# An FFN of one selected row inside a fused attention kernel: gate, up and h brought to 128 partitions by small DMAs instead of matmuls, the down rows regrouped to fit, and the row chosen two units sooner

## The chip, the cores and the metric

The kernel runs on one core of one Trainium2 chip. The metric is the device time of one execution in microseconds (us). A "unit" below is one tile of 8 matmuls of 512 columns on the matrix engine (PE): 8 x 0.216 = 1.73 us (in the kernel before, 16 such matmuls take 3.45 us from 44.52 to 47.97 us). DVE is the vector engine, ACT the scalar engine, POOL the GpSimd engine and SP the engine that issues most DMAs.

## The reference, cut to what matters

```python
# x: [1, 2048, 1024]; w_gate, w_up: [1024, 3584]; w_down: [3584, 1024]; all bf16
r = x @ w_r                                   # one router logit for each of 2048 tokens
idx = argsort(-r)[:, :1]                      # C = 1: one token is chosen
x_sel = take_along_axis(x, idx)
y = (silu(x_sel @ w_gate) * (x_sel @ w_up)) @ w_down
b = x + scatter(y * sigmoid(r[idx]))          # only the chosen row gets y
a = linear_attention(x, wqkv) @ wo            # 32 heads, phi(t) = where(t > 0, t + 1, exp(t)) + 1e-6
g = sigmoid((x * gate_w).sum(-1))
out = g * a + (1 - g) * b
```

Nearly all the arithmetic is attention on PE. The FFN works on one row, but has to read 22 MB of weights. So it is laid beside the attention: DVE and PE use the weights while PE goes through the key, value and query units.

Of the kernel before, what the change touches and what calls it, by code (L numbers as in the profile page):

```python
# [13 lines left out]
BF = mybir.dt.bfloat16  # L14
# [8 lines left out]
P = 128  # L23
# [10 lines left out]
GU_AFTER = {(7, "end"): 4, (9, 1): 4, (10, 3): 8, (12, 1): 8}  # L34
FLUSH_AFTER = {(9, 3), (13, 0)}
GATE_STEPS = {6: 5, 7: 6, 8: 5}
M_AFTER = {3: (0, 0), 6: (0, 1), 9: (1, 0), 12: (1, 1)}
DOWN_STEPS = {10: (1, 1, 1, 1, 1, 1), 11: (1, 1, 1, 1, 1), 12: (1, 0, 1, 1, 1), 13: (1, 1, 1, 1, 1), 14: (1, 1, 1, 1, 1), 15: (1, 1, 1)}
# [5 lines left out]
def kernel(  # L44
# [113 lines left out]
    sel4 = const.tile([P, 4], BF)  # L158
    nc.gpsimd.memset(sel4[:], 0.0)
    for j in range(4):  # L160
        nc.gpsimd.memset(sel4[32 * j : 32 * j + 1, j : j + 1], 1.0)
# [212 lines left out]
    h_bf = [rt.tile([P, 512], BF, name=f"h_bf{i}") for i in range(2)]  # L374
    sg_t = [rt.tile([P, 512], F32, name=f"sg{i}") for i in range(2)]
# [14 lines left out]
    def finish_gate(half, ps, w):  # L390
        eg = tmp.tile([P, 512], F32, tag="ffn_e", bufs=1)
        act.activation(eg[:, 0:w], ps[:, 0:w], ACTF.Exp, scale=-1.0)
        dve.tensor_scalar_add(eg[:, 0:w], eg[:, 0:w], 1.0)
        dve.reciprocal(eg[:, 0:w], eg[:, 0:w])
        dve.tensor_tensor(sg_t[half][:, 0:w], ps[:, 0:w], eg[:, 0:w], op=ALU.mult)

    def finish_up(half, ps, w):
        dve.tensor_tensor(h_bf[half][:, 0:w], ps[:, 0:w], sg_t[half][:, 0:w], op=ALU.mult)

        def h_transpose():  # L400
            hps = ps_ffn.tile([P, 16], F32, tag="f")
            nb = w // P
            for b in range(nb):
                pe.matmul(hps[:, 4 * b : 4 * b + 4], lhsT=h_bf[half][:, b * P : (b + 1) * P], rhs=sel4[:], start=True, stop=True)
            dst = hcol[:].rearrange("p (j b) -> p j b", b=7)[:, :, 4 * half : 4 * half + nb]
            src = hps[:, 0 : 4 * nb].rearrange("p (b j) -> p j b", j=4)
            dve.tensor_copy(dst, src)

        ffn_state["pending"] = h_transpose

    def gate_up(half, which):
        w = 512 if half == 0 else 384
        for wi in which:
            wmat = (B_w_gate, B_w_up)[wi]
            for c in range(KC):
                def load(wmat=wmat, c=c):
                    return gate_up_load(half, wmat, c)

                def compute(wt, wi=wi, c=c):
                    if c == 0:  # L420
                        ps = ps_ffn.tile([P, 512], F32, tag="f")
                        ffn_state["ps"] = ps
                    ps = ffn_state["ps"]
                    for j in range(4):
                        pe.matmul(ps[32 * j : 32 * j + 32, 0:w], lhsT=xs_pad[:, c, :], rhs=wt[:, w * j : w * j + w],
                                  start=(c == 0), stop=(c == KC - 1), tile_position=(0, 32 * j))
                    if c == KC - 1:
                        (finish_gate, finish_up)[wi](half, ps, w)

                yield load, compute  # L430
# [15 lines left out]
    def gate_reduce():  # L446
# [4 lines left out]
        finish_gate(0, ps, 512)  # L451

    def down_rows():
        wdv = B_w_down.rearrange("(k p) n -> p k n", p=P)
        pairs = [(7 * j + b, 1) for b in (0, 2) for j in range(4)]
        pairs += [(7 * j + 4, 1) for j in range(4)] + [(6, 7), (20, 7)]
        for i2, (k0, dk) in enumerate(pairs):
            def load(k0=k0, dk=dk):
                wt = ffw.tile([P, 2048], BF, tag="ffw")
                ld = nc.sync.dma_start(out=wt[:].rearrange("p (k n) -> p k n", k=2), in_=wdv[:, k0 : k0 + dk + 1 : dk, :])  # L460
# [4 lines left out]
            def compute(wt, kk, i2=i2, k0=k0, dk=dk):  # L465
                w, h1 = wt[:, 1024 * kk : 1024 * kk + 1024], hcol[:, k0 + dk * kk : k0 + dk * kk + 1]
                if i2 == 0 and kk == 0:
# [26 lines left out]
    def ffn_pieces():  # L494
# [5 lines left out]
        for n in (2, 4):  # L500
            yield from islice(dn, n)
            yield from islice(gu, 8)
# [4 lines left out]
    inflight = deque()  # L507

# [6 lines left out]

    def ffn_flush():
        pend = ffn_state.pop("pending", None)
        if pend is not None:
            pend()
# [33 lines left out]

    q_units = deque((g, j) for j in range(4) for g in range(NG))
    for t in range(4):
        unit_KVACC(t)
    for t in range(4, NT):
        for nb in range(4):
# [4 lines left out]
            ffn_step(GU_AFTER.get((t, nb), 0))  # L563
            if (t, nb) in FLUSH_AFTER:
                ffn_flush()
            gate_step(int(nb < GATE_STEPS.get(t, 0)))
            steps = DOWN_STEPS.get(t, ())
            if nb < len(steps):
                down_step(steps[nb])
        for i in range(Q_PER_T[t]):  # L570
            unit_Q(*q_units.popleft())
            gate_step(int(4 + i < GATE_STEPS.get(t, 0)))
            if 4 + i < len(steps):
                down_step(steps[4 + i])
            if t == 4 and i == 0:
                router_part1()
                ffn_prefetch()
        if t == 5:
            router_part2()
        ffn_step(GU_AFTER.get((t, "end"), 0))  # L580
# [167 lines left out]
```

## The kernel before: what the change and the argument touch

One ring of nine 512 KB buffers (`FFN_DEPTH`) takes all the FFN's weights in the order of `ffn_pieces`; a new load is issued when a buffer is free. DVE accumulates the gate's half 0 and all the down rows by scaled adds (`gate_step`, `down_step`, half a buffer at a time); PE does the other gate and up pieces in groups of four or eight (`ffn_step`). Constants say after which unit of the attention what is done. "Half 0" has 4 x 512 of the 3584 hidden columns and "half 1" 4 x 384.

```python
GU_AFTER = {(7, "end"): 4, (9, 1): 4, (10, 3): 8, (12, 1): 8}
FLUSH_AFTER = {(9, 3), (13, 0)}
GATE_STEPS = {6: 5, 7: 6, 8: 5}
DOWN_STEPS = {10: (1, 1, 1, 1, 1, 1), 11: (1, 1, 1, 1, 1), 12: (1, 0, 1, 1, 1), 13: (1, 1, 1, 1, 1), 14: (1, 1, 1, 1, 1), 15: (1, 1, 1)}
FFN_DEPTH = 9
# ... (cut)
    def finish_gate(half, ps, w):          # silu of 128 x w, of whose partitions only 0, 32, 64, 96 matter
        eg = tmp.tile([P, 512], F32, tag="ffn_e", bufs=1)
        act.activation(eg[:, 0:w], ps[:, 0:w], ACTF.Exp, scale=-1.0)
        dve.tensor_scalar_add(eg[:, 0:w], eg[:, 0:w], 1.0)
        dve.reciprocal(eg[:, 0:w], eg[:, 0:w])
        dve.tensor_tensor(sg_t[half][:, 0:w], ps[:, 0:w], eg[:, 0:w], op=ALU.mult)

    def finish_up(half, ps, w):
        dve.tensor_tensor(h_bf[half][:, 0:w], ps[:, 0:w], sg_t[half][:, 0:w], op=ALU.mult)

        def h_transpose():                 # h to 128 partitions by 4 (half 0) or 3 (half 1) matmuls
            hps = ps_ffn.tile([P, 16], F32, tag="f")
            nb = w // P
            for b in range(nb):
                pe.matmul(hps[:, 4 * b : 4 * b + 4], lhsT=h_bf[half][:, b * P : (b + 1) * P], rhs=sel4[:], start=True, stop=True)
            # ... (cut: copy of hps to hcol on DVE)
        ffn_state["pending"] = h_transpose
# ... (cut)
    def down_rows():
        wdv = B_w_down.rearrange("(k p) n -> p k n", p=P)          # row 128k + p on partition p
        pairs = [(7 * j + b, 1) for b in (0, 2) for j in range(4)]
        pairs += [(7 * j + 4, 1) for j in range(4)] + [(6, 7), (20, 7)]
        for i2, (k0, dk) in enumerate(pairs):
            def load(k0=k0, dk=dk):
                wt = ffw.tile([P, 2048], BF, tag="ffw")
                ld = nc.sync.dma_start(out=wt[:].rearrange("p (k n) -> p k n", k=2), in_=wdv[:, k0 : k0 + dk + 1 : dk, :])
                # ... (cut: order of the queue)
                return wt

            def compute(wt, kk, i2=i2, k0=k0, dk=dk):
                w, h1 = wt[:, 1024 * kk : 1024 * kk + 1024], hcol[:, k0 + dk * kk : k0 + dk * kk + 1]
                if i2 == 0 and kk == 0:
                    dve.tensor_scalar(yacc, w, h1, None, op0=ALU.mult)
                else:
                    dve.scalar_tensor_tensor(yacc, w, h1, yacc, op0=ALU.mult, op1=ALU.add)

            yield load, compute
# ... (cut)
    def ffn_pieces():
        g0, u0, gu, dn = gate_rows(), gate_up(0, (1,)), gate_up(1, (0, 1)), down_rows()
        yield from islice(g0, 6)
        yield from islice(u0, 4)
        yield from g0
        yield from u0
        for n in (2, 4):                   # down pieces ahead of each group of half 1
            yield from islice(dn, n)
            yield from islice(gu, 8)
        yield from dn
        yield from wo_pieces()
# ... (cut)
    for t in range(4, NT):
        for nb in range(4):
            unit_KV(t, nb)
            # ... (cut)
            ffn_step(GU_AFTER.get((t, nb), 0))
            if (t, nb) in FLUSH_AFTER:
                ffn_flush()                # the pending h_transpose
            gate_step(int(nb < GATE_STEPS.get(t, 0)))
            steps = DOWN_STEPS.get(t, ())
            if nb < len(steps):
                down_step(steps[nb])
        for i in range(Q_PER_T[t]):
            unit_Q(*q_units.popleft())
            # ... (cut: further steps)
            if t == 4 and i == 0:
                router_part1()             # DVE: index of the row; POOL: fetch of the row
                ffn_prefetch()
        if t == 5:
            router_part2()                 # PE: the row to 128 partitions
        ffn_step(GU_AFTER.get((t, "end"), 0))
        if t == 8:
            gate_reduce()
```

A unit's result leaves its bank of PE's accumulator memory through ACT and then, for a key or a query, through one DVE instruction (`pk` or `pq_all` in the trace). There are four such banks (`ps_work`, `bufs=4`).

## Time and profile before

| | kernel before |
|---|---|
| time, median of 3 runs | 251.46 us (251.42 to 251.52) |
| span of the profiled run | 250.1 us |
| PE busy, granted clock | 244.7 us (98%), 1.00 |
| DVE, ACT, POOL busy | 163.1, 125.8, 51.9 us |
| PE's waits in the whole span | 1.7 us |

PE bounds the kernel; the prediction below shows the lines for that. Here are the page's line of DMA shares in 40 slices (tenths of all 16 DMA engines' time; a slice is 6.25 us), its line on the down loads (14 loads of 512 KB, median 5.8 us from issue to landing), and from the list of waits DVE's wait for down rows (us in total, times, longest):

```profile
DMA  6999990019999928499699996230000564454122
...
wt<-in_B_w_down_dram SPq DMA_DIRECT2D x14, 512.0 KB, 5.8
...
DVE gacc L80 <- DMA wt<-in_B_w_down_dram: 3.7, 3, 1.8
```

The table of windows gives the rate while down rows are loading. Its columns are the stretch, its length, the busy time and count of PE, PEld, DVE, ACT and POOL, then PE's clock, the DMA share and GB/s:

```profile
130.00:135.00 5.00, 5.00 (x28) 2.27 (x27) 4.38 (x7) 3.59 (x6) 1.06 (x2) 1.00 1.05 301
```

The share is at 1.05: all 16 engines work, at a mean of 301 GB/s, and a piece of 512 KB takes 524,288 bytes / 301 GB/s = 1.7 us. By their packets, about 57 of the 301 GB/s are loads of `A_wo` issued by POOL; without them it is 244 GB/s, or 2.1 us a piece. DVE needs a piece every two units, 3.5 us, so the stream is clearly faster than its use and DVE waits only 3.7 us in all.

### The profile page before, as it was taken

Reading aid. Unit: us, or ns where it says so; the run is one execution under the profiler, and the core shown is the slowest. Engines: PE = TensorE matmul, PEld = TensorE weight load, DVE = VectorE, ACT = ScalarE, POOL = GpSimd, SP = SyncE. Lnnn points to the kernel's source line nnn. Section 1 sums busy time; section 2 is a strip of 40 time slices with the busy share of each in tenths; the row PEclk is TensorE's granted clock in tenths of the full one; section 3 lists DMA queues with packets and bytes.
Section 4 is the critical chain, followed back from the end, with each engine's and each line's share of the span. In section 5 each row is a group of like instructions: output and inputs, shape, how many; then the busy total and the mean of one; then the engine's idle time right before and its main releaser. Section 6 shows DMA issues by size and latency. Waiting matters only on the chain.

```text
span 250.1 us, 4197 instructions
## 1 busy us (share of the span) xinstructions
PE 244.7 (98%) x1602; PEld 111.1 (44%) x1602; DVE 163.1 (65%) x257; ACT 125.8 (50%) x200; POOL 51.9 (21%) x102
## 2 busy tenths in 40 slices
PE   7999999999999999999999999999999999999994
PEld 3444454444444434444544444444444444444442
DVE  0045015326999288699689993585878999953442
ACT  2096235556545364564535554568887633333210
POOL 5000001010000100000132000210666689950000
PEclk9999999999999999999999999999999999999999
DMA  6999990019999928499699996230000564454122
GB/s 199 303 340 225 258 334 26 0 27 320 350 348 272 340 58 250 146 338 327 194 292 300 457 349 134 70 132 1 3 0 5 171 210 144 161 175 144 66 84 84
DMA packets 47242, 47.73 MB, mean 191 GB/s; under 512 B 18732, under 2 KB 35380, under 8 KB 47160
## 3 DMA queue, kind: packets, MB, share of 16 engines
q1 hardware_dynamic: 46552, 46.29, 60.7%
q0 software_dynamic: 640, 1.19, 1.8%
q8 instruction: 12, 0.20, 0.3%
q14 instruction: 6, 0.05, 0.1%
q10 hardware_dynamic: 32, 0.00, 0.0%
HBM read 39.34 MB, written 8.40 MB: 191 GB/s over the span
## 4 chain that ended last, share of the span: by engine, by line
PE 95%; DMA 2%; SPq 1%; DVE 0%; issue 0%; DVEq 0%
PE ps L80 88%; PE first L80 2%; DMA wkv<-in_A_wqkv_dram 2%; PE kvacc L80 2%; PE dps L80 1%; PE rps L80 1%; SPq L80 1%; PE pm L80 1%; PE gps L80 0%; DVE ot L80 0%; PE yps L80 0%; PE xs_ps L80 0%; DVEq L743 0%; PE pt L80 0%; PE hps L80 0%
## 5 line engine op out<-in xcount | busy, mean ns | idle before, releaser
L80 PE MATMUL ps<-wkv,xT 128*128 128x512 bf16 x480 | 106.5, 379 | 0.0
L80 PEld LDWEIGHTS <-xT 128*128 128x128 bf16 x512 | 49.3, 98 | 60.5 <-issue 2.6
L80 PE MATMUL ps<-xT,wq 128*128 128x512 bf16 x256 | 58.4, 379 | 0.0
L80 PE MATMUL ps<-m_sb,pq_all 128*128 128x512 bf16 (+2 forms) x264 | 55.6, 373 | 0.0
L80 ACT ACTIVATE u<-ps 128x512 f32<-128x512 f32 x60 | 35.9, 599 | 36.5 <-PE ps L80 35.8
L80 ACT ACTIVATE e<-u 128x512 f32<-128x512 f32 x64 | 40.4, 632 | 2.0
L646 POOL TENSOR_TENSOR pq_all<-pq_all,rb 128x512 bf16<-128x512 bf16 x32 | 36.6, 1163 | 14.4 <-DVE rb L80 13.9
L80 PEld LDWEIGHTS <-pq_all 128*128 128x128 bf16 x264 | 25.5, 98 | 30.2 <-issue 0.4
L80 PEld LDWEIGHTS <-wq 128*128 128x128 bf16 x256 | 24.3, 98 | 30.2 <-issue 2.1
L80 DVE SCALAR_TENSOR_TENSOR pq_all<-ps,e 128x512 bf16<-128x512 f32 x32 | 22.0, 686 | 23.6 <-ACT e L80 23.5
L80 DVE SCALAR_TENSOR_TENSOR gacc<-wt,hcol,gacc 128x1024 f32<-128x1024 bf16 x27 | 34.6, 1281 | 4.1 <-DMA wt<-in_B_w_down_dram 3.7
L80 ACT CAST vt<-ps 128x512 bf16<-128x512 f32 x32 | 18.9, 589 | 32.8 <-PE ps L80 32.8
L80 DVE SCALAR_TENSOR_TENSOR ot<-ps,gate,xg 128x512 bf16<-128x512 f32 (+2 forms) x33 | 23.6, 724 | 15.1 <-PE ps L80 14.2
L80 ACT ACTIVATE xg<-xt,omg 128x1024 f32<-128x1024 bf16 x16 | 18.2, 1148 | 25.8 <-DVE ot L80 25.8
L80 DVE SCALAR_TENSOR_TENSOR pk<-ps,e 128x512 bf16<-128x512 f32 x28 | 19.1, 686 | 7.5 <-ACT e L80 7.5
L209 POOL MEMSET vt<- 128x16 bf16 x16 | 2.4, 200 | 101.8 <-PE kvacc L80 101.3
L80 DVE STREAM_SHUFFLE rb<-rdp 128x512 f32<-128x512 f32 x32 | 22.5, 731 | 0.0
L80 DVE SCALAR_TENSOR_TENSOR gacc<-wt,xs_f,gacc 128x1024 f32<-128x1024 bf16 x14 | 17.4, 1283 | 0.3 <-DMA wt<-in_B_w_gate_dram 0.3
L80 DVE CAST r_bf<-rps 128x512 bf16<-128x512 f32 x1 | 0.7, 692 | 12.6 <-PE rps L80 12.6
L80 DVE SCALAR_TENSOR_TENSOR pk<-first,e 128x512 bf16<-128x512 f32 x4 | 2.8, 692 | 8.4 <-ACT e L80 8.4
L80 PE MATMUL first<-wkv,xT 128*128 128x512 bf16 x32 | 7.4, 379 | 0.2
L80 DVE RECIPROCAL rd<-dn 128x512 f32<-128x512 f32 x2 | 6.7, 3334 | 0.0
(104 smaller groups left out, 88.1 us busy)
## 6 DMA issues: line engine op xcount, KB each, us to landing
wt<-in_B_w_down_dram SPq DMA_DIRECT2D x14, 512.0 KB, 5.8
wt<-in_B_w_gate_dram SPq DMA_DIRECT2D x8, 512.0 KB, 7.2
wt<-in_B_w_up_dram SPq DMA_DIRECT2D x8, 512.0 KB, 8.9
xt<-xp SPq DMA_DIRECT2D x16, 256.0 KB, 2.9
out_dram<-ot SPq DMA_DIRECT2D x15, 256.0 KB, 2.0
wt<-in_B_w_gate_dram SPq DMA_DIRECT2D x8, 384.0 KB, 5.3
wt<-in_B_w_up_dram SPq DMA_DIRECT2D x8, 384.0 KB, 7.5
wkv<-in_A_wqkv_dram SPq DMA_DIRECT2D x8, 256.0 KB, 5.2
```

The costliest lines, as they stand in the source:

```text
L80: inst = fn(*a, **k)
L209: nc.gpsimd.memset(vt_t[t][:, :, :, 64:65], 1.0)
L646: nc.gpsimd.tensor_tensor(sl, sl, rb[:], op=ALU.mult)
```

## The change

Its intent: relieve DVE of the work on 128x512 tiles of which four rows matter, and PE of the seven small transposing matmuls. The rows of gate and up are copied out by ACT, four small DMAs bring them to 128 partitions x 16 (or 12) columns, and silu and the product run on those. A column f of h then stands at another place, so each buffer of down rows has to hold other rows: partition 32j + r takes the rows of column group j that stand together in one stretch of memory. The row is chosen two units sooner, and the plan of steps is shifted to match. The diff, cut to its core:

```diff
-GU_AFTER = {(7, "end"): 4, (9, 1): 4, (10, 3): 8, (12, 1): 8}
-FLUSH_AFTER = {(9, 3), (13, 0)}
-GATE_STEPS = {6: 5, 7: 6, 8: 5}
+GU_AFTER = {(7, 3): 4, (8, "end"): 4, (10, 3): 8, (12, 1): 8}
+GATE_STEPS = {5: (0, 1, 1, 1, 1), 6: (1, 1, 1, 1, 1), 7: (1, 1, 1, 0, 1, 1), 8: (1, 1)}
-DOWN_STEPS = {10: (1, 1, 1, 1, 1, 1), 11: (1, 1, 1, 1, 1), 12: (1, 0, 1, 1, 1), 13: (1, 1, 1, 1, 1), 14: (1, 1, 1, 1, 1), 15: (1, 1, 1)}
+DOWN_STEPS = {9: (0, 0, 0, 1, 1), 10: (1, 1, 0, 0, 1, 1), 11: (1, 1, 1, 1), 12: (0, 0, 1, 1, 1), 13: (1, 1, 1, 1, 2), 14: (1, 1, 1, 1, 1), 15: (1, 1, 1, 1)}
+FINISH_AT = {(9, 2), (11, 0), (12, 4)}
... (cut: finish_gate, finish_up and h_transpose go; sel4 goes)
+    def finish(wi, half, ps):
+        w = 512 if half == 0 else 384
+        n = w // 32
+        act.copy(rows[wi][:, 0:w], ps[:, 0:w])
+        nc.gpsimd.dma_start(out=cols[half][wi][:, 0:n], in_=rows[wi][0:128:32, 0:w])
+        g, u, h = cols[half][0][:, 0:n], cols[half][1][:, 0:n], slice(16 * half, 16 * half + n)
+
+        def silu():
+            e = rt.tile([P, 16], F32, name=f"ffn_e{half}")
+            act.activation(e[:, 0:n], g, ACTF.Exp, scale=-1.0)
+            dve.tensor_scalar_add(e[:, 0:n], e[:, 0:n], 1.0)
+            dve.reciprocal(e[:, 0:n], e[:, 0:n])
+            dve.tensor_tensor(g, g, e[:, 0:n], op=ALU.mult)
+
+        def product():
+            dve.tensor_tensor(h_bf[:, h], u, g, op=ALU.mult)
+            dve.tensor_copy(hcol[:, h], h_bf[:, h])
+
+        late.append((silu, product)[wi])
... (cut)
     def down_rows():
-        wdv = B_w_down.rearrange("(k p) n -> p k n", p=P)
-        pairs = [(7 * j + b, 1) for b in (0, 2) for j in range(4)]
-        pairs += [(7 * j + 4, 1) for j in range(4)] + [(6, 7), (20, 7)]
-        for i2, (k0, dk) in enumerate(pairs):
-            def load(k0=k0, dk=dk):
+        wdv = B_w_down.rearrange("(j f) n -> j f n", j=4)
+        for k in range(0, 28, 2):
+            c0, n, i0 = (0, 16, k) if k < 16 else (512, 12, k - 16)
+
+            def load(c0=c0, n=n, i0=i0):
                 wt = ffw.tile([P, 2048], BF, tag="ffw")
-                ld = nc.sync.dma_start(out=wt[:].rearrange("p (k n) -> p k n", k=2), in_=wdv[:, k0 : k0 + dk + 1 : dk, :])
+                src = wdv[:, c0 : c0 + 32 * n, :].rearrange("j (r i) n -> j r i n", i=n)[:, :, i0 : i0 + 2, :]
+                ld = nc.sync.dma_start(out=wt[:], in_=src.rearrange("j r i n -> j r (i n)"))
... (cut: compute, with hcol's column k + kk)
-        for n in (2, 4):
+        for n in (2, 3):
             yield from islice(dn, n)
             yield from islice(gu, 8)
... (cut: a helper that does the steps of a slot and the late parts of the FFN at FINISH_AT; router_part1 after KV(4,1), router_part2 after KV(5,0))
```

More of the change, by code (lines that the diff above doesn't have):

```diff
@@ L157 @@
     nc.gpsimd.memset(ones_row[:], 1.0)
-    sel4 = const.tile([P, 4], BF)
-    nc.gpsimd.memset(sel4[:], 0.0)
-    for j in range(4):
-        nc.gpsimd.memset(sel4[32 * j : 32 * j + 1, j : j + 1], 1.0)
     off16_i = const.tile([P, 1], I32)
@@ L373 @@
     ffw = phq.enter_context(tc.tile_pool(name="ffw", bufs=FFN_DEPTH, side="right"))
-    h_bf = [rt.tile([P, 512], BF, name=f"h_bf{i}") for i in range(2)]
-    sg_t = [rt.tile([P, 512], F32, name=f"sg{i}") for i in range(2)]
+    rows = [rt.tile([P, 512], F32, name=f"gu_rows{i}") for i in range(2)]
+    cols = [[rt.tile([P, 16], F32, name=f"gu_cols{i}{h}") for i in range(2)] for h in range(2)]
+    h_bf = rt.tile([P, 28], BF)
     ffn_state = {}
@@ L388, in gate_up_load @@
         return wt
-    def finish_gate(half, ps, w):
-        eg = tmp.tile([P, 512], F32, tag="ffn_e", bufs=1)
-        act.activation(eg[:, 0:w], ps[:, 0:w], ACTF.Exp, scale=-1.0)
-        dve.tensor_scalar_add(eg[:, 0:w], eg[:, 0:w], 1.0)
-        dve.reciprocal(eg[:, 0:w], eg[:, 0:w])
-        dve.tensor_tensor(sg_t[half][:, 0:w], ps[:, 0:w], eg[:, 0:w], op=ALU.mult)
-    def finish_up(half, ps, w):
-        dve.tensor_tensor(h_bf[half][:, 0:w], ps[:, 0:w], sg_t[half][:, 0:w], op=ALU.mult)
-        def h_transpose():
-            hps = ps_ffn.tile([P, 16], F32, tag="f")
-            nb = w // P
-            for b in range(nb):
-                pe.matmul(hps[:, 4 * b : 4 * b + 4], lhsT=h_bf[half][:, b * P : (b + 1) * P], rhs=sel4[:], start=True, stop=True)
-            dst = hcol[:].rearrange("p (j b) -> p j b", b=7)[:, :, 4 * half : 4 * half + nb]
-            src = hps[:, 0 : 4 * nb].rearrange("p (b j) -> p j b", j=4)
-            dve.tensor_copy(dst, src)
-        ffn_state["pending"] = h_transpose
+    def finish(wi, half, ps):
[14 more added lines that the diff above has]
+        late.append((silu, product)[wi])
     def gate_up(half, which):
@@ L427, in compute @@
                     if c == KC - 1:
-                        (finish_gate, finish_up)[wi](half, ps, w)
+                        finish(wi, half, ps)
                 yield load, compute
@@ L450, in gate_reduce @@
                       start=True, stop=True, tile_position=(0, 32 * j))
-        finish_gate(0, ps, 512)
+        finish(0, 0, ps)
+        late.rotate(1)
     def down_rows():
-        wdv = B_w_down.rearrange("(k p) n -> p k n", p=P)
-        pairs = [(7 * j + b, 1) for b in (0, 2) for j in range(4)]
-        pairs += [(7 * j + 4, 1) for j in range(4)] + [(6, 7), (20, 7)]
-        for i2, (k0, dk) in enumerate(pairs):
-            def load(k0=k0, dk=dk):
+        wdv = B_w_down.rearrange("(j f) n -> j f n", j=4)
+        for k in range(0, 28, 2):
+            c0, n, i0 = (0, 16, k) if k < 16 else (512, 12, k - 16)
+            def load(c0=c0, n=n, i0=i0):
                 wt = ffw.tile([P, 2048], BF, tag="ffw")
-                ld = nc.sync.dma_start(out=wt[:].rearrange("p (k n) -> p k n", k=2), in_=wdv[:, k0 : k0 + dk + 1 : dk, :])
+                src = wdv[:, c0 : c0 + 32 * n, :].rearrange("j (r i) n -> j r i n", i=n)[:, :, i0 : i0 + 2, :]
+                ld = nc.sync.dma_start(out=wt[:], in_=src.rearrange("j r i n -> j r (i n)"))
                 tc.add_manual_dep(ld.ins, ffn_state["last_ld"].ins.name, NOSYNC, reason="queue order")
@@ L463, in load, with compute @@
                 return wt
-            def compute(wt, kk, i2=i2, k0=k0, dk=dk):
-                w, h1 = wt[:, 1024 * kk : 1024 * kk + 1024], hcol[:, k0 + dk * kk : k0 + dk * kk + 1]
-                if i2 == 0 and kk == 0:
+            def compute(wt, kk, k=k):
+                w, h1 = wt[:, 1024 * kk : 1024 * kk + 1024], hcol[:, k + kk : k + kk + 1]
+                if k + kk == 0:
                     dve.tensor_scalar(yacc, w, h1, None, op0=ALU.mult)
@@ L507 @@
     inflight = deque()
+    late = deque()
     def ffn_prefetch():
@@ L514, in ffn_prefetch @@
             inflight.append((nxt[0](), nxt[1]))
-    def ffn_flush():
-        pend = ffn_state.pop("pending", None)
-        if pend is not None:
-            pend()
     def ffn_step(n):
@@ L552, in down_finish, with slot @@
                             in_=brow[0:128:32, :])
+    def slot(t, i):
+        gu = GU_AFTER.get((t, i), 0)
+        ffn_step(gu)
+        strict[0] = True
+        while late and (t, i) in FINISH_AT:
+            late.popleft()()
+        strict[0] = False
+        for step, plan in ((gate_step, GATE_STEPS), (down_step, DOWN_STEPS)):
+            steps = plan.get(t, ())
+            if i != "end" and i < len(steps):
+                step(steps[i])
     q_units = deque((g, j) for j in range(4) for g in range(NG))
@@ L562 @@
                     unit_KVACC(t0)
-            ffn_step(GU_AFTER.get((t, nb), 0))
-            if (t, nb) in FLUSH_AFTER:
-                ffn_flush()
-            gate_step(int(nb < GATE_STEPS.get(t, 0)))
-            steps = DOWN_STEPS.get(t, ())
-            if nb < len(steps):
-                down_step(steps[nb])
+            if (t, nb) == (4, 1):
+                router_part1()
+                ffn_prefetch()
+            if (t, nb) == (5, 0):
+                router_part2()
+            slot(t, nb)
         for i in range(Q_PER_T[t]):
             unit_Q(*q_units.popleft())
-            gate_step(int(4 + i < GATE_STEPS.get(t, 0)))
-            if 4 + i < len(steps):
-                down_step(steps[4 + i])
-            if t == 4 and i == 0:
-                router_part1()
-                ffn_prefetch()
-        if t == 5:
-            router_part2()
-        ffn_step(GU_AFTER.get((t, "end"), 0))
+            slot(t, 4 + i)
+        slot(t, "end")
         if t == 8:
```

## The prediction

> **What bounds the kernel now.** I read the page's busy shares and slices first, then the list of what the matrix engine (PE) waited for, then the timeline of PE alone, then the groups of the vector engine (DVE). The first two parts of the page:
>
> ```profile
> PE 244.7 (98%) x1602; PEld 111.1 (44%) x1602; DVE 163.1 (65%) x257; ACT 125.8 (50%) x200; POOL 51.9 (21%) x102
> ...
> PE   7999999999999999999999999999999999999994
> ...
> DVE  0045015326999288699689993585878999953442
> ...
> PEclk9999999999999999999999999999999999999999
> ```
>
> PE is busy in every slice, DVE has whole slices near full (9) beside slices at half. The granted clock is full throughout. Busy alone is not proof, so the second view is the waits of PE over the whole span:
>
> ```profile
> PE warm_ps L80 <- PEq L732: 1.0, 1, 1.0
> PE pst L80 <- DMA xnat<-in_A_x_dram: 0.7, 1, 0.7
> ```
>
> That is all: 1.7 us, both before 6.2 us. From 6.9 us to the last matmul near 246.3 us PE never waits. The FFN part that is changed (44 to 157 us) lies wholly inside this stretch. So time can only be gained by giving PE less to do, and lost by making PE wait. The timeline of PE alone shows what the FFN costs it:
>
> ```profile
> 72.56 3.62 PE L80 MATMUL ps<-xT,wq 128*128 128x512 bf16 x16
> 76.10 1.05 PE L80 MATMUL ps<-wt,xs_pad 128*32 128x512 bf16 x16
> 77.08 3.63 PE L80 MATMUL ps<-wkv,xT 128*128 128x512 bf16 x16
> ...
> 85.25 1.89 PE L80 MATMUL ps<-xT,wq 128*128 128x512 bf16 x8
> 87.07 1.06 PE L80 MATMUL gps<-gacc,ones_f 128*32 128x512 f32 x8
> 88.07 3.63 PE L80 MATMUL ps<-wkv,xT 128*128 128x512 bf16 x16
> 91.62 1.05 PE L80 MATMUL ps<-wt,xs_pad 128*32 128x512 bf16 x16
> ...
> 96.07 0.24 PE L80 MATMUL hps<-sel,h_bf 128*128 128x4 bf16 x4
> 96.17 1.89 PE L80 MATMUL ps<-xT,wq 128*128 128x512 bf16 x8
> ...
> 131.43 0.22 PE L80 MATMUL hps<-sel,h_bf 128*128 128x4 bf16 x3
> 131.50 5.34 PE L80 MATMUL ps<-wkv,xT 128*128 128x512 bf16 x24
> ```
>
> Read starts, not durations, because the durations overlap. The four transposing matmuls hold PE from 96.07 to 96.17, the three from 131.43 to 131.50: 0.10 + 0.07 = 0.17 us (the chain that ended last gives them 0.08 + 0.05 = 0.13).
>
> The dear part of the old FFN stands on DVE, from the groups of DVE by shape:
>
> ```profile
> L80 DVE RECIPROCAL eg<-eg 128x512 f32<-128x512 f32 x1 | 3.4, 3353 | 0.0
> ...
> L80 DVE RECIPROCAL eg<-eg 128x384 f32<-128x384 f32 x1 | 2.6, 2554 | 0.0
> ```
>
> And the small DMAs that are there already, from the page's last part as the fuller answer on DMA gives it:
>
> ```profile
> c<-cand POOLq DMA_DIRECT2D x1, 0.0 KB, 1.8
> xsel_row<-in_A_x_dram POOLq DMA_DIRECT2D x1, 2.0 KB, 2.5
> ```
>
> [...] the 16 matmuls from 44.52 to 47.97 us take 3.45 / 16 = 216 ns each. [...] 8 query matmuls ahead of a 128x32-tiled group take 87.07 - 85.25 = 1.82 us, against 8 x 0.216 = 1.73 elsewhere, and 16 take 3.54 in place of 3.45. A visit to the tiled mode costs about 0.09 us. [...] 3353 ns for 512 columns against 417 ns for the add of one on the same tile. [...] The trace has 1.7 to 2.5 us for the three small ones here.
>
> **The change, part by part.**
> (a) Transposing matmuls go: 7 matmuls, 0.13 to 0.17 us off PE. On the bounding engine, so all of it counts. I take 0.15.
> (b) The work on 128x512 rows goes from DVE: exp's add 0.42 + 0.35, reciprocals 3.35 + 2.55, products 0.68 + 0.55 (gate) and 0.68 + 0.55 (h), copies to hcol 0.18 + 0.16: 9.5 us. In its place come per half an add, a reciprocal, a product, the h product and a copy on 16 or 12 columns. Rows of that size take 0.15 to 0.25 us in this trace (the gate's 128x16 add 0.166, reciprocal 0.247): about 5 x 0.17 x 2 = 1.7 us. DVE loses some 7.8 us of 163. It lies beside PE, which never waits for DVE, so it is worth 0.
> (c) ACT: two exps (0.58 + 0.49) become four row copies (2 x 0.59 + 2 x 0.49, taking the copy of 128x512 at 0.588) and two exps of about 0.2: about +1.5 us on an engine busy 50%. Worth 0.
> (d) Four small DMAs, issued from GpSimd, each about 0.7 us of issue and 1.8 to 2.5 us to landing. After each there is room: the gate and up rows of half 0 are consumed three units (3 x 1.73 = 5.2 us) after the reduction ends near 89 us. Copy 0.6 + issue and landing 2.5, with the first DMA's issue ahead of the second 0.7, makes 3.8 us, so landing near 93 against use near 95. Half 1's gate has two query units and one KV unit (5.2 us), its up product two KV units and a query (5.2 us), each needing about 3. Worth 0 unless a landing is more than 1.5 us late, and then still first a delay of ACT and DVE, not of PE: four work banks of 1.73 us stand between.
> (e) Order: the up group moves from 91.62 to the end of t = 8, directly ahead of the gate reduction. Both are 128x32-tiled, so one visit to the tiled mode is saved: 0.09 us. The first up group, now two query units sooner, keeps its own visit. I count 0.09.
> (f) Row choice sooner: the DVE chain that ran from 48.35 (behind the first query unit) to 49.47 moves behind KV(4,1), whose DVE part ended at 43.25, so to about 44.35. Its input landed at 39.98 + 1.8 = 41.8, no wait. The row's fetch started 51.06 - 49.47 = 1.6 after the chain: 45.95, and lands at 45.95 + 2.5 = 48.45. PE needs it after KV(5,0), which ends at 47.97 + 1.73 = 49.70. Margin 1.25 us, so the 9 tiny matmuls move from 56.70 to about 49.7 with no stall. The weight stream starts near 48.7 in place of 53.79, its first piece lands near 53.4, and the first gate step wants it near 53.7 (4.66 us from issue to first use, as before).
> (g) Down rows: 14 loads of 512 KB as before, but each partition reads two consecutive rows, 4 KB together in place of 2 x 2 KB. Same bytes, fewer packets. One down piece now comes after the second up group, so the copy to xp and the gate logits behind it are queued about 1 us later. Their results are first used at 157 us on ACT, which then sits idle 2.2 us. Worth 0.
> Sum: -0.15 - 0.09 = -0.24 us. 251.46 - 0.24 = **251.2 us**, which is 0.1% faster.
>
> **Rivals.** *A wait takes the place of the matmuls.* The scarcest margin is (f): if the fetch lands 2 us later than before (contention, a slower register load), PE waits about 0.7 us: 252. For it speaks that the margin is only 1.25 us; against it that the DMA engines moved 0 GB/s from 44 to 52 us. The same could happen in (d): the small DMAs share the engines with the weight stream, and the loads from GpSimd of 128 KB had a median of 7.0 us there against 2.8 from the sync queue. A landing at 7 us would put DVE and ACT 2 to 3 us behind; they have 4 banks of slack, so at most 1 us reaches PE: 252.2. *DVE was the hidden bound* and 7.8 us of relief speeds the kernel: that would make up to 247 us, but PE shows no wait for DVE in the whole trace, even from 90 to 95 us where DVE was busy all 5.00 us. I give it 1%. *The weight stream becomes the bound*, as buffers (nine) are now released in another order: before, the stream ran at 340 to 360 GB/s from 60 to 75 us and left PE no wait; with a start 5 us sooner and the consumption of the first groups 2 units (3.5 us) sooner the margin grows by 1.5 us. If a group of eight pieces were late after all, PE would stand for 1 to 3 us: 252.5 to 254.5. Some 4%. *The transfers are hidden anyway and so is the saving*: this is the base case, with only the PE terms left.
>
> **Range and chances.** The three runs before spread by 0.1 us, so the range comes from the stalls: no stall gives 251.1 to 251.4; one small stall 251.7 to 252.2. [...] Range 250.8 to 252.0. A gain over 2% needs 5.0 us off PE, which does nothing removable of that size: 1%. A loss over 2% needs stalls of 5 us: 1.5%. Within 2%: 97.5%.
>
> **What the new profile should show.** No transposing matmuls; up group and gate reduction adjacent near 87 to 89 us; the row's matmuls near 49.7 with no idle; the first weight load at about 48.7; DVE busy near 155, ACT near 127, PE near 244.5; the list of PE's waits still only the two at the start; four new small DMAs with about 2 us to landing. The prediction is wrong if PE waits for the selected row, for weight pieces, or for a bank held behind DVE or ACT.

## The result

| | before | after |
|---|---|---|
| time, median of 4 runs each | 251.49 us (251.42 to 251.59) | 296.52 us (294.81 to 297.24) |
| span of the profiled run | 250.1 us | 294.8 us |
| PE busy | 244.7 us | 251.7 us |
| mean granted clock | 1.000 | 0.947 |
| PE's waits for DVE | none | 38.1 us |
| DVE's waits for down rows | 3.7 us | 49.4 us |

The ratio after to before is 1.178, with a 95% interval of 1.173 to 1.183: 17.8% slower. A ratio here and below is the mean time of one kernel's fast runs over that of the other's of the same rounds, so it is not quite the ratio of the medians. The prediction said 251.2 us and a range up to 252.0 (its lower end, 250.8, was the author's estimate); it was wrong by 45 us.

The page of the changed kernel has, in its busy shares and its 40 slices (now of 7.4 us each), the answer to the lines of before:

```profile
PE 251.7 (85%) x1595; PEld 112.3 (38%) x1595; DVE 156.7 (53%) x257; ACT 127.0 (43%) x204; POOL 54.0 (18%) x101
...
PE   7999999998999993299722746759999999999995
...
PEclk9999999999999999589995897959999999999999
DMA  7999913999758245583124329725400036445312
...
PE 56%; DMA 32%; DVE 6%; issue 3%; SPq 1%; ACT 0%; POOLq 0%; DVEq 0%; POOL 0%
```

PE has holes from the 16th to the 27th slice (about 110 to 199 us), the granted clock falls in six slices there, and the DMA share is at 1 to 5 tenths in most of them. Yet the chain that ended last (the last line) runs through DMA for 32% of the span, against 2% before. So the kernel waits for transfers while the DMA engines are mostly idle. The list of waits says who waits for what (of the 33.9 us in its second line, the first 0.81 us, at 71.2 us, stand behind gate rows, the rest behind down rows):

```profile
DVE gacc L80 <- DMA wt<-in_B_w_down_dram: 49.4, 12, 9.4
...
PE ps L80 <- DVE pq_all L80: 33.9, 5, 11.2
...
PE ps L80 <- DVE pk L80: 4.2, 3, 1.9
```

The order of cause is to be read from the top: DVE waits for down rows, and PE for DVE. How a wait goes over from the one to the other shows in the timelines of PE and of DVE around 150 us. First PE (start, length, engine, line, operation and how many; in brackets the idle time before and who ended it):

```profile
143.95 5.34 PE L80 MATMUL ps<-wkv,xT 128*128 128x512 bf16 x24
160.47 3.57 PE L80 MATMUL ps<-wkv,xT 128*128 128x512 bf16 x8 [11.19 <-DVE pq_all L80]
```

Then DVE:

```profile
151.95 2.61 DVE L80 SCALAR_TENSOR_TENSOR gacc<-wt,hcol,gacc 128x1024 f32<-128x1024 bf16 x2 [8.05 <-DMA wt<-in_B_w_down_dram]
157.21 2.61 DVE L80 SCALAR_TENSOR_TENSOR gacc<-wt,hcol,gacc 128x1024 f32<-128x1024 bf16 x2 [2.66 <-DMA wt<-in_B_w_down_dram]
159.74 0.68 DVE L80 SCALAR_TENSOR_TENSOR pq_all<-ps,e 128x512 bf16<-128x512 f32 x1
```

The `pq_all` at 159.74 needs nothing of the FFN. It would free a bank of PE, but it stands behind four down steps, and those wait for their rows. PE has filled its four banks by 149.3 and stands for 11.2 us until `pq_all` has run. The window table of this stretch shows what the transfers are doing meanwhile (columns as above):

```profile
150.00:155.00 5.00, 0.00 (x0) 0.00 (x0) 2.57 (x2) 0.00 (x0) 0.15 (x1) 0.94 0.25 102
155.00:160.00 5.00, 0.00 (x0) 0.00 (x0) 2.75 (x3) 0.00 (x0) 0.90 (x2) 0.50 0.38 133
```

The share is 0.25, as much as 4 engines of 16 would make, and the rate is 102 GB/s, where it was 301 before, 244 of them for down rows. A piece now takes 524,288 bytes / 102 GB/s = 5.1 us, and DVE needs one every 3.5 us. The second line has PE's clock at 0.50, and it stays there when PE goes on: the 8 matmuls at 160.47 us take 3.57 us at 0.50, where the 8 at 142.15 us take 1.89 at 1.00. The same shows after the other three stalls of over 5 us (10.25 us to 123.67, 6.18 to 179.04 and 5.43 to 195.30): behind each of the four PE works for 2.6 to 3.6 us at 0.50, 12.9 us in all. Half of that, 6.4 us, is an estimate of what the slow clock has in PE's additional busy time, 251.7 - 244.7 = 7.0 us.

Together: waits 38.1 + busy 7.0 = 45.1 us; the spans differ by 294.8 - 250.1 = 44.7 us.

The other parts of the change do show as intended. PE's timeline at the selected row, and at the up group and the gate reduction:

```profile
49.20 0.35 PE L80 MATMUL xs_ps<-one_bf,xsel_row 1*128 1x1 bf16 x8
...
87.44 1.05 PE L80 MATMUL ps<-wt,xs_pad 128*32 128x512 bf16 x16
88.32 1.03 PE L80 MATMUL gps<-gacc,ones_f 128*32 128x512 f32 x8
89.28 7.08 PE L80 MATMUL ps<-wkv,xT 128*128 128x512 bf16 x32
```

And the small DMAs (KB each, median us from issue to landing):

```profile
gu_cols<-gu_rows POOLq DMA_DIRECT2D x2, 8.0 KB, 5.7
gu_cols<-gu_rows POOLq DMA_DIRECT2D x2, 6.0 KB, 4.9
...
xsel_row<-in_A_x_dram POOLq DMA_DIRECT2D x1, 2.0 KB, 1.7
```

### The profile page after: what moved, and what is told of

Read it like the earlier page. It is cut to its first block, busy times and chain, and to the rows that moved or that the text cites. A ratio compares the mean times of both kernels' runs of the same rounds, so it can differ in the third digit from the quotient of the medians.

```text
span 294.8 us, 4190 instructions
## 1 busy us (share of the span) xinstructions
PE 251.7 (85%) x1595; PEld 112.3 (38%) x1595; DVE 156.7 (53%) x257; ACT 127.0 (43%) x204; POOL 54.0 (18%) x101
## 2 busy tenths in 40 slices
DMA packets 45410, 47.76 MB, mean 162 GB/s; under 512 B 18676, under 2 KB 35332, under 8 KB 45328
## 4 chain that ended last, share of the span: by engine, by line
PE 56%; DMA 32%; DVE 6%; issue 3%; SPq 1%; ACT 0%; POOLq 0%; DVEq 0%; POOL 0%
PE ps L80 51%; DMA wt<-in_B_w_down_dram 26%; DMA wt<-in_B_w_gate_dram 4%; DVE gacc L80 3%; PE first L80 2%; DMA wkv<-in_A_wqkv_dram 1%; DVE pk L80 1%; PE kvacc L80 1%; PE dps L80 1%; PE rps L80 1%; DMA xsel<-in_A_x_dram 1%; PE pm L80 0%; DVE pq_all L80 0%; SPq L80 0%; PE gps L80 0%
## 5 line engine op out<-in xcount | busy, mean ns | idle before, releaser
L80 PE MATMUL ps<-wkv,xT 128*128 128x512 bf16 x480 | 113.6, 395 | 33.9 <-DVE pq_all L80 33.9
L80 PEld LDWEIGHTS <-xT 128*128 128x128 bf16 x512 | 50.9, 100 | 99.2 <-issue 44.1
L80 DVE SCALAR_TENSOR_TENSOR gacc<-wt,hcol,gacc 128x1024 f32<-128x1024 bf16 x27 | 34.6, 1283 | 49.8 <-DMA wt<-in_B_w_down_dram 49.4
L80 ACT ACTIVATE u<-ps 128x512 f32<-128x512 f32 x60 | 35.8, 597 | 40.3 <-PE ps L80 40.1
L80 PEld LDWEIGHTS <-pq_all 128*128 128x128 bf16 x264 | 25.5, 98 | 30.2 <-issue 0.4
L80 DVE SCALAR_TENSOR_TENSOR ot<-ps,gate,xg 128x512 bf16<-128x512 f32 (+2 forms) x33 | 24.2, 748 | 15.0 <-PE ps L80 14.2
L80 DVE STREAM_SHUFFLE rb<-rdp 128x512 f32<-128x512 f32 x32 | 23.2, 765 | 0.0
L484 POOL DMA_DIRECT2D wt<-in_A_wo_dram x8 | 4.3, 542 | 25.8 <-DVE gacc L80 25.8
L391 POOL DMA_DIRECT2D gu_cols<-gu_rows x4 | 2.7, 687 | 25.4 <-ACT gu_rows L80 25.3
```

Of the source, the lines that this page charges most:

```text
L80: inst = fn(*a, **k)
L391: nc.gpsimd.dma_start(out=cols[half][wi][:, 0:n], in_=rows[wi][0:128:32, 0:w])
L484: ld = eng.dma_start(out=wt[32 * r : 32 * r + 32, :].rearrange("p (c n) -> p c n", c=2), in_=wo_v[k // 2, r][:, 2 * (k % 2) : 2 * (k % 2) ...
```

## The experiments

**The theory, A.** The theory is that the outermost dimension of a down load's source sets how many of the 16 DMA engines work on it. The new source is the pattern [4][32][2048] (j, r, then i and n together), so its outermost dimension is 4, and only 4 engines would work, whatever the destination's 128 partitions. The trace of the changed kernel agrees so far: 0.25 of 16 engines is 4, and the share stays at 0.25 with several down loads queued at once; what goes above it near 156 and 162 us (up to 0.85 and 0.99 in half a microsecond) comes 1 to 2 us after POOL issued loads of `A_wo` (at 154.85 and 160.11 us), which are other DMAs. 102 GB/s / 4 = 25.5 GB/s an engine.

The share alone could also be 16 engines that are each busy a quarter of the time. The DMA packets kept with the traces speak against that. In the changed kernel, from 150 to 155 us, at least four data packets are under way for 99.8% of the time, and exactly four for 91%; a packet of 4 KB takes 162 ns in the median, which is 25.3 GB/s. The traces do not name the engine of a packet.

**The rivals.** The runs of 4 KB in place of 2 KB could be slow in themselves. Or the new plan (order of pieces, of steps, the small DMAs) starves DVE whatever the source is. Or a part comes from each. In the expectations A is the theory above and D is the rival by which a part comes from the rest of the change; where other letters stand, they are the other rivals.

Several of these kernels bring rows of the down weights to the wrong columns of h: the bytes, the buffers and the work stay the same. It changes one row of 2048, and the comparison with the reference proves little for them; it is said with each whether its rows are right. Kernels that were run together share the runs of the kernel before.

| run | what it is | us, median (range, runs) | before | ratio (95%) |
|---|---|---|---|---|
| e2 | before, source with 4 outermost | 291.10 (288.59 to 291.43, 5) | 251.38 | 1.158 (1.155 to 1.160) |
| e3 | before, 8 outermost | 262.58 (261.31 to 265.08, 4) | 251.38 | 1.048 (1.041 to 1.055) |
| e5 | before, 16 outermost | 254.24 (253.08 to 256.05, 4) | 251.38 | 1.013 (1.008 to 1.019) |
| e8 | after, the old source | 255.28 (255.05 to 255.71, 4) | 251.63 | 1.014 (1.013 to 1.016) |
| e7 | after, 4 KB runs, 128 outermost | 256.62 (254.87 to 256.85, 6) | 251.63 | 1.017 (1.015 to 1.020) |
| e1 | after, each load as four DMAs | 268.14 (267.28 to 269.53, 4) | 251.38 | 1.068 (1.064 to 1.073) |
| e12 | e1 with pinned order | 264.64 (263.86 to 265.50, 4) | 251.69 | 1.051 (1.047 to 1.054) |
| e4 | after, regrouped, 128 outermost | 254.37 (251.92 to 255.18, 6) | 251.63 | 1.008 (1.004 to 1.013) |
| e9 | e8 with the old down plan | 252.24 (251.06 to 252.74, 6) | 251.75 | 1.001 (0.999 to 1.003) |
| e10 | e4 with the old down plan | 251.26 (250.90 to 251.60, 6) | 251.75 | 0.998 (0.997 to 1.000) |

**e2, e3, e5: the outermost dimension alone, in the kernel before.** Nothing but the source of the down loads is changed, to patterns of the same 512 KB in runs of 4 KB (rows wrong):

```diff
-        wdv = B_w_down.rearrange("(k p) n -> p k n", p=P)
+        wdv = B_w_down.rearrange("(j m r i) n -> m j r (i n)", j=4, m=14, i=2)   # e2; e3: j=8; e5: j=16
...
-                ld = nc.sync.dma_start(out=wt[:].rearrange("p (k n) -> p k n", k=2), in_=wdv[:, k0 : k0 + dk + 1 : dk, :])
+                ld = nc.sync.dma_start(out=wt[:], in_=wdv[i2])
```

Expected of e2, then e3, then e5:

> The kernel before with only the down loads' source changed: pairs of adjacent rows (4 KB runs) with an outermost dimension of 4; wrong result on purpose (rows permuted against h), all else as before, no small DMA. Theory A: each 512 KB piece takes 512 KB / 102 GB/s = 5.1 us on 4 engines against 3.46 us of PE work per piece, so the kernel becomes as slow as the changed one, 280 to 305 us, with a DMA share of 0.25 where only down loads run. Rival B (row strides of the change): here the 32 rows of a block lie together, so 251 to 254 us. Rival C: no small DMAs, 251.5 us.

> As e2 but with an outermost dimension of 8. Wrong result on purpose. Theory A: 8 of 16 engines, about 204 GB/s, 2.6 us per piece, under the 3.46 us of PE work per piece, so most of the loss goes: 251.5 to 258 us, DMA share about 0.5 where only down loads run. Rival B (4 KB runs of adjacent rows are slow): as slow as e2.

> As e2 but with an outermost dimension of 16, the control for run length and addresses. Wrong result on purpose. Theory A: all 16 engines, so 251.2 to 251.8 us, DMA share about 1 in the stretch of down loads. Rival B (4 KB runs): as slow as e2.

Measured: with 4 outermost the old kernel takes 291.10 us, nearly as long as the changed one; DVE waits 40.9 us for down rows in 11 waits. The window table of e2 where only down loads run:

```profile
108.00:112.00 4.00, 3.95 (x20) 1.80 (x19) 1.10 (x1) 2.73 (x5) 0.00 (x0) 1.00 0.25 102
```

The same share of 0.25 and the same 102 GB/s, in a kernel that has no other part of the change. With 8 outermost the time is 262.58 us, 4.6 us above what was expected; DVE waits 14.6 us, and PE itself 4.5 us for up rows, which the expectation did not reckon with. The single microseconds in which nearly all packets are those of down loads (130 to 133 and 135 to 138 us) have shares near 0.5 (0.49 to 0.57). Two of them:

```profile
131.00:132.00 1.00, 0.48 (x5) 0.14 (x5) 0.00 (x0) 0.00 (x0) 0.00 (x0) 0.50 0.49 184
136.00:137.00 1.00, 1.00 (x7) 0.41 (x6) 1.00 (x2) 0.10 (x1) 0.00 (x0) 1.00 0.51 205
```

With 16 the share is 1.04 and the wait is 8.1 us. The packets say the same: of data packets, mostly 4 are under way at once in e2 (108 to 112 us), 8 in e3 (131 to 133), 16 in e5 (126 to 131). So the three steps of 4, 8 and 16 engines come out as A says, and the first two shares were not to be had from any rival.

e5 missed its expectation, though, by 2.4 us. Its window, against the 301 GB/s of the kernel before in the same stretch:

```profile
130.00:135.00 5.00, 5.00 (x27) 2.33 (x26) 4.93 (x7) 2.83 (x5) 1.96 (x4) 1.00 1.04 241
```

All engines are busy and yet deliver a fifth less, and in the single microseconds from 126 to 137 us e5 stays at 217 to 258. The kernel before, read in the same way, changes between two rates at full share: 405 GB/s from 126 to 128 us, 234 from 128 to 131, 390 from 131 to 133, 241 from 136 to 138. So a rate near 240 is nothing new, only that e5 does not have the other in this stretch. A packet of 4 KB takes 276 ns there (126 to 131 us), against 162 in e2. Loads of `A_wo` run beside the down loads in most of the old kernel's slow stretches, but they are not the cause in e5, which has none of their packets from 126 to 132 us. Which addresses give which rate was not tried; the cause is open.

**e8: the change without its source.** The whole changed kernel, only with the source pattern of before (rows wrong). The order of the instructions on each engine was compared with that of the changed kernel and is the same:

```diff
-        wdv = B_w_down.rearrange("(j f) n -> j f n", j=4)
+        wdv = B_w_down.rearrange("(k p) n -> p k n", p=P)
...
-                src = wdv[:, c0 : c0 + 32 * n, :].rearrange("j (r i) n -> j r i n", i=n)[:, :, i0 : i0 + 2, :]
-                ld = nc.sync.dma_start(out=wt[:], in_=src.rearrange("j r i n -> j r (i n)"))
+                ld = nc.sync.dma_start(out=wt[:].rearrange("p (k n) -> p k n", k=2), in_=wdv[:, k : k + 2, :])
```

> The changed kernel with only the source of the down loads put back to that of the kernel before (outermost dimension 128, two runs of 2 KB per partition); the order of instructions on every engine is that of the changed kernel. Rows no longer fit h, wrong on purpose. Theory A (4 of 16 engines is the whole cause of the loss): 251.0 to 252.3 us, the waits of DVE for down rows gone, at most the one new wait of 0.8 us of PE near 71 us left. Rival C (small DMAs, order): above 285 us. Rival D (part of the loss, as the 17 us left with four transfers per piece, comes of the rest of the change): 258 to 270 us.

Measured: 255.28 us, above the range of A and below that of D. Of the 45 us, 41 are gone with this one access pattern. DVE's wait for down rows falls from 49.4 us to this:

```profile
DVE gacc L80 <- DMA wt<-in_B_w_down_dram: 9.5, 3, 4.2
```

The other 3.7 us are still there, so A is not the whole cause, and the rest of the change costs something too. The waits show where. First DVE's timeline, then PE's:

```profile
131.13 5.25 DVE L80 SCALAR_TENSOR_TENSOR gacc<-wt,hcol,gacc 128x1024 f32<-128x1024 bf16 x4 [4.18 <-DMA wt<-in_B_w_down_dram]
```

```profile
137.04 2.48 PE L80 MATMUL ps<-wkv,xT 128*128 128x512 bf16 x8 [2.45 <-DVE pq_all L80]
```

DVE has run dry just behind the second group of half 1. The program says why: that group takes eight of the nine buffers at once, and the next down loads can be issued only as it frees them. The old order of pieces has six down pieces ahead of it, the new one five, so the new plan had to leave DVE fewer steps (10 of 28, in place of 12) before the gap. Four steps then stand in a row at 131.13, and PE waits 2.45 us for the `pq_all` behind them, after which its clock is at 0.50 from 138.2 to 141.6 us. The wait and half of these 3.4 us make 4.2 us, an estimate that is near the 3.7 lost.

**e7: the 4 KB runs without the 4.** The changed kernel with the down rows read as 128 partitions of consecutive rows (rows wrong):

```diff
-        wdv = B_w_down.rearrange("(j f) n -> j f n", j=4)
+        wdv = B_w_down.rearrange("(p i) n -> p i n", i=28)
...
-                src = wdv[:, c0 : c0 + 32 * n, :].rearrange("j (r i) n -> j r i n", i=n)[:, :, i0 : i0 + 2, :]
-                ld = nc.sync.dma_start(out=wt[:], in_=src.rearrange("j r i n -> j r (i n)"))
+                src = wdv[:, k : k + 2, :]
+                ld = nc.sync.dma_start(out=wt[:], in_=src.rearrange("p i n -> p (i n)"))
```

> The changed kernel with only the source of the down loads changed: outermost dimension 128, one run of 4 KB per partition, partitions 56 KB apart. Wrong on purpose, order of instructions unchanged. Theory A with runs of 4 KB costing nothing: same as with the old source, 251 to 252.3 us. Theory A with runs of 4 KB slower (about 240 GB/s against 310 GB/s, as the run with an outermost dimension of 16 shows): 2 to 5 us above the old source, 253 to 257 us.

Measured: 256.62 us, about 1.3 us more than e8 in the medians, with ranges that overlap. Runs of 4 KB are not what made the changed kernel slow.

**e1 and e12: the right rows by four DMAs.** Each load of the changed kernel is divided by j into four DMAs of 32 partitions, whose outermost dimension is 32 (rows right):

```diff
-                ld = nc.sync.dma_start(out=wt[:], in_=src.rearrange("j r i n -> j r (i n)"))
+                for j in range(4):
+                    ld = nc.sync.dma_start(out=wt[32 * j : 32 * j + 32, :], in_=src[j].rearrange("r i n -> r (i n)"))
```

> The changed kernel with each down load issued as four transfers of 32 partitions each in place of one whose source's outermost dimension has 4 entries; same bytes, same rows, same 4 KB runs, right result. Theory A (a transfer with an outermost dimension of 4 runs on 4 of the 16 DMA engines only): the down loads use all engines again, DVE's 49 us of waiting for down rows shrinks to under 6 us, the time falls to 251 to 253 us. Rival B (the strided row addresses or the 4 KB runs make the reads slow): the addresses are the same, so the time stays above 285 us. Rival C (the new small DMAs and their waits on ACT and DVE hold the pipeline): nothing of them is changed, above 285 us.

Measured: 268.14 us. DVE's wait for down rows is down to 3.2 us in one wait, as A says, but the time missed the expectation by 15 us or more. DVE's timeline near the end of the FFN, and PE's longest wait in the list of waits:

```profile
162.85 10.52 DVE L80 SCALAR_TENSOR_TENSOR gacc<-wt,hcol,gacc 128x1024 f32<-128x1024 bf16 x8
```

```profile
PE yps L80 <- DVE gacc L80: 8.7, 1, 8.7
```

Eight down steps stand in one block at the end, and PE waits 8.7 us for the last. Outside the marked parts the program leaves the order of DVE's instructions to the build, which had ordered them otherwise for this kernel than for the changed one. So e1 changes two things at once. In its trace the loss is nearly all at this place: DVE goes through the block without waiting for a row, PE's next longest wait is 3.6 us, right behind, and its clock is at 0.50 from 167.9 to 181.6 us. e12 was to mend that by asking for program order from t = 9 on:

```diff
     def slot(t, i):
+        strict[0] = t >= 9
...
-        strict[0] = False
+        strict[0] = t >= 9
... (and back to False behind down_finish)
```

> The run with four transfers of 32 partitions per down piece, with the program order of the tensor, vector and scalar engines pinned from t = 9 to the end of the FFN (in the first such run the scheduler had put 8 of the 28 down steps behind the query unit after the last KV accumulation, and PE waited 8.7 us there). Right result. Theory: what was left of that run's loss (268 us) came of this order, so with the order pinned it comes down to that of the run with long runs on one transfer, 254 to 259 us. Rival: four transfers of 32 partitions are themselves slower in delivery, then it stays above 264 us with DVE waiting for down rows.

Measured: 264.64 us, above the 254 to 259 us expected and just inside the rival's range, though DVE waits only 5.2 us for down rows. The order was once more another one (down steps behind the closing of the key-value sums, the last of those sums split up), with waits of up to 2.2 us spread over PE and its clock at 0.50 from 167.7 to 178.0 us. The pair stays inconclusive on how much of its 13 to 17 us is order and how much slower delivery: in e1 the down loads came at 224 to 239 GB/s with all engines busy (a share of 1.02 to 1.06 from 130 to 145 us).

**e4: a regrouping that keeps 128 outermost.** Half 0 is given the columns 0 to 2047 and half 1 the rest, in place of a part of each of four column groups. Then partition p takes n rows that stand together, and the pattern is [128][2048]; the gate and up pieces become one run of 4 KB (3 KB) for each row, in place of four of 1 KB (rows right):

```diff
     def gate_up_load(half, wmat, c):
-        w, c0 = (512, 0) if half == 0 else (384, 512)
+        w, c0 = (512, 0) if half == 0 else (384, 2048)
...
+        ld = nc.sync.dma_start(out=wt[:, 0 : 4 * w], in_=wmat[c * P : (c + 1) * P, c0 : c0 + 4 * w])
...
     def down_rows():
         for k in range(0, 28, 2):
+            r0, n, i0 = (0, 16, k) if k < 16 else (2048, 12, k - 16)
...
+                src = B_w_down[r0 : r0 + P * n, :].rearrange("(p i) n -> p i n", i=n)[:, i0 : i0 + 2, :]
+                ld = nc.sync.dma_start(out=wt[:], in_=src.rearrange("p i n -> p (i n)"))
```

> A right version of the change: half 0 takes columns 0 to 2047 and half 1 columns 2048 to 3583, so that the down rows of all 128 partitions have one stride and the load has an outermost dimension of 128; gate and up loads become one run of 4 KB or 3 KB per partition. Order of instructions unchanged. Theory A: 251 to 254 us. If long runs are slower, gate and up loads suffer too and it is slower than the run with 4 KB runs in the down loads alone: 254 to 262 us.

Measured: 254.37 us, 0.4 us above A's range, with 2.3 us of PE's waits for DVE left. So the intent of the change is to be had with full transfers (a share of 1.01 at 316 GB/s from 130 to 135 us).

**e9 and e10: the second cause.** e8 and e4 with the old number of pieces and the steps to fit it (e9 rows wrong, e10 rows right):

```diff
-DOWN_STEPS = {..., 11: (1, 1, 1, 1), 12: (0, 0, 1, 1, 1), 13: (1, 1, 1, 1, 2), 14: (1, 1, 1, 1, 1), 15: (1, 1, 1, 1)}
+DOWN_STEPS = {..., 11: (1, 1, 1, 1, 1), 12: (1, 0, 1, 1, 1), 13: (1, 1, 1, 1, 1), 14: (1, 1, 1, 1, 1), 15: (1, 1, 1)}
...
-        for n in (2, 3):
+        for n in (2, 4):
```

> The changed kernel with the old source of the down loads, and besides with four down pieces between the two groups of half 1 in place of three (and the step plan to fit: 12 of 28 steps ahead of the second group in place of 10). Wrong on purpose, as before. Theory D1 (the 3.7 us left with the old source come of one down piece fewer in flight when the second group holds eight of nine buffers, so DVE runs dry near 127 us and PE waits 2.5 us and loses clock): 251.1 to 252.0 us, DVE's waits for down rows fall from 9.5 to about 4 us and PE has no wait of over 0.5 us in the FFN stage. Rival D2 (the rest comes of the small DMAs or of the row choice): stays at 254 to 256 us.

> The right version with regrouped columns (load sources with an outermost dimension of 128) and four down pieces between the two groups. Theory D1: 250.9 to 252.0 us, that is what was predicted for the change, 0.1 to 0.2 us under the kernel before if the count of matmuls and of tiled visits is right. Rival D2: 253 to 255 us.

Measured: e9 takes 252.24 us, 0.2 us above D1's range and far below D2's; e10 takes 251.26 us, inside D1's range. In e9 DVE still waits 5.7 us for down rows, where about 4 were expected, and PE was to have no wait over 0.5 us. e9's longest wait of PE left is 1.3 us at 71.5 us, behind gate rows that came late to DVE. e10, whose gate and up loads run at 398 GB/s from 50 to 65 us, does not have that one. Its list of PE's waits is down to this:

```profile
PE warm_ps L80 <- PEq L728: 1.0, 1, 1.0
PE ps L80 <- issue: 0.5, 3, 0.2
```

Against the kernel before of the same rounds e10's ratio is 0.9983, with an interval from 0.9967 to 0.9999. By the measure of 2% that is the same time; the interval, which ends just below 1, speaks for a gain of some 0.2%.

## Why the prediction was wrong, point by point

**The step that failed is (g).** It put the down rows as "14 loads of 512 KB as before, but each partition reads two consecutive rows, 4 KB together in place of 2 x 2 KB. Same bytes, fewer packets", worth 0. Bytes and packets were right (45,410 packets against 47,242). What it did not look at is the outermost dimension of the new source. The diff shows it in the letters of the last rearrangement, "j r i n -> j r (i n)" with j = 4. In its place the runs showed a share of 0.25, as of 4 engines of 16, 102 GB/s and 5.1 us a piece against a need of one in 3.5 us. The trace of the changed kernel agrees with that size: from 151.95 to 192.04 us seven down pieces are waited for one after another, 40.1 / 7 = 5.7 us each. e2 shows it alone in the old kernel (+39.7 us), e8 takes it alone out of the new one (-41.2 us).

**The second half of (g)** failed too: "One down piece now comes after the second up group" was also put at 0, because only the copy behind it was looked at and not the buffers ahead of it. With the number of pieces and the steps put back together, it was worth 252.24 against 255.28 us, so 3.0 us (e9 and e8), and 254.37 against 251.26, so 3.1 us (e4 and e10).

**The rival was named, and mis-sized.** "The weight stream becomes the bound" was in the prediction, for 1 to 3 us and at 4%. It took the rate of the stream from before (340 to 360 GB/s) for a source that had changed. From 102 GB/s the same sum would have said that DVE falls behind by 5.1 - 3.5 = 1.6 us a piece once the buffers are empty. For 14 pieces that is at most 22 us (an estimate): far above the range, and still only half of the loss. The slowed clock adds some 6.4 us of PE time (the estimate above); how the rest came about was not divided further.

**The four banks** did not hold what they were trusted with. The prediction let DVE be "2 to 3 us behind", with four banks of 1.73 us between. DVE was up to 9.4 us behind in one wait, and four banks are 6.9 us. The longest stall of PE was 11.2 us.

**The clock** was not in the prediction at all. It fell to 0.50 in each of the four stalls of over 5 us, and PE's busy time grew by 7.0 us. In the stall that began at 149.3 us it is still at 1.00 up to 154.3, with PE idle, and at 0.50 from 154.5. e8 shows that the stall need not be so long: there the clock is halved from 138.2 us, after PE had stood for only 2.45 us and was at work again since 137.04. After the stall of 1.90 us that ended at 142.15 us in the changed kernel it stayed at 1.00.

**What held.** (f): the selected row's matmuls are at 49.20 us (predicted near 49.7) without a wait, the first weight load at 47.65 (48.7), the row's landing took 1.7 us; PE ran 0.6 us ahead of the old trace even before the row was chosen (the query units at 43.93 against 44.52 us). (e) and (a): up group and gate reduction are adjacent at 87.44 and 88.32, 89.28 - 87.44 = 1.84 us for both, and no transposing matmul is left. In the kernel before, the two groups took 1.00 us (87.07 to 88.07) and 0.98 us (91.62 to 92.60) apart, so standing together saves 0.14 us more, besides the 0.09 predicted for (e): an up group takes 0.98 us ahead of an untiled unit and 0.88 (87.44 to 88.32) ahead of the reduction. e10, with PE's waits for DVE gone, is 0.5 us under the kernel before in the medians, where -0.24 us was predicted; the 0.14 accounts for a part, and e10 has other gate and up loads as well, so it is no pure measure of (a) and (e). (b) and (c): DVE is busy 156.7 us (predicted near 155), ACT 127.0 (127).

**(d) was right in its worth and wrong in its sizes.** The small DMAs took 5.7 and 4.9 us to landing in the median of two (those of half 0 ran with a DMA share of 0.96 from 89.6 to 95.5 us; those of half 1, alike but for the time, took 7.0 us at 107 us and 2.9 us at 137 us; what they waited for is not shown), in e10 6.2 and 5.7, where 2 to 2.5 was predicted from those that run while the weight stream is not there. ACT waited 2.0 us for them in the changed kernel, 1.4 in e10. PE did not wait in e10, so the worth of 0 stands.

**What stays open:** why the same number of engines delivers near 240 or near 400 GB/s for down rows at different addresses, and how the loss of e1 and e12 divides into order and delivery.

## What to carry to other kernels

When a load is regrouped, write down the outermost dimension of its source as the DMA gets it, not only bytes and run lengths: here 4 in place of 128 took the rate of the down rows from 244 to 102 GB/s, and the old access pattern alone gave back 41 of 45 us. A DMA share that stands at a fraction, as here at 0.25, while someone waits for that DMA (DVE for 49.4 us) is the sign to look for. And ask of each piece in a ring of buffers how many pieces are ahead of a group that takes nearly the whole ring; what ran dry on DVE here reached PE, the bounding engine, through the results that queued behind it (38.1 us of waits).
